# First batch's loads of a rotary attention and feed-forward kernel: 26 transfers where there were 56

## The chip, the cores and the metric

The kernel runs on one core of a Trainium2 chip. The core has a matrix engine (TensorE, PE in the profile), a vector engine (VectorE, DVE), a scalar engine (ScalarE, ACT), GpSimd (POOL) and a queue engine (SyncE, SP) that starts nearly all transfers between the chip's memory and the on-chip memory; 16 DMA engines carry them out. The metric is the device time of one execution in microseconds (us), the median of three runs.

## The reference

Attention with rotated q and k over 4 batches, 8 heads, 576 positions and 64 columns, then a feed-forward layer on the 2304 rows of 512:

```python
def rotate(x):
    x1, x2 = (x[..., :half], x[..., half:])
    return np.concatenate([x1 * cos - x2 * sin, x1 * sin + x2 * cos], axis=-1)
q_rot, k_rot = (rotate(q), rotate(k))
scores = scale * np.matmul(q_rot, k_rot.transpose(0, 1, 3, 2))
scores = scores - np.max(scores, axis=-1, keepdims=True)
attn = np.exp(scores)
attn = attn / (np.sum(attn, axis=-1, keepdims=True) + 1e-09)
attn_out = np.matmul(attn, v)              # then heads side by side: x
h = x @ w_in                               # 512 to 2048
g = h * (1.0 / (1.0 + np.exp(-h)))
out = g @ w_out                            # 2048 to 512
```

All inputs and the output are 32-bit floats. The kernel splits most operands of the matrix engine into a high and a low half-precision part and adds the products.

## The kernel before, in words

The heads of a batch are taken in four pairs, p = 0 to 3. Batches 1 to 3 are split into two half-precision parts and turned by transposing transfers. The first batch goes another way, so that the matrix engine has work early: its q and k are rotated as 32-bit products with the sine and the cosine table (`product`, two instructions for the first 512 positions and one for the last 64 of each table), and the matrix engine turns both products and adds them (`tr`). Its v is needed in two forms: as 32-bit blocks for the first half of the queries (`first_v`, read by `fpv` in `add_pv_first`), and as half-precision parts (`hi`, `lo_first`) for the second half.

The 512 positions are laid out four to a partition, so their transfer is one instruction for two heads; the last 64 positions of each head take transfers of their own. `add_qk_first` issues six transfers for a pair (q, its two last blocks, k, its two last blocks), `add_v` three for v, and `add_v_first` three more for v's second copy: 12 for each of the four pairs. The two rotation tables take four each, the 512 positions twice, so that both heads have a copy. That makes 56.

The weights come in 16 pieces of rows, are rounded by a chain ACT, POOL or ACT, DVE (`fT`, `fC`, `fX`: L811, L813, L819), and their sums of squares give the scales (`trace`, L357 on the matrix engine). The first piece is loaded before anything else, the second behind the tables.

What runs when is written out by hand: `ORDER` is one list of numbered steps, each with the letter of its engine (s for SP's queue). Every engine works through its own steps in that order, and an instruction that waits holds up all behind it on its engine. SP's queue runs eight transfers at a time: each further one waits until the one eight before it has landed. Buffers come from rotating pools (`TAGS`): `rt` and `n` have two each, `io` two, `ob` four, `Tk2` four. Until a weight's place is used for the weight, q, k and v of the first pairs lie in it (`x_place`).

The lines that matter here: L448 and L453 load q and k, L657 to L662 and L628 to L633 load v, L420 and L422 load the tables, L473 and L475 are the rotation's products, L487 to L497 the turning, L813 and L819 the rounding of a weight.

Of the kernel before, what the change touches and what calls it, by code (L numbers as in the profile page):

```python
# [14 lines left out]
ALU = mybir.AluOpType  # L15
# [5 lines left out]
STREAM = (0,)  # L21

# [16 lines left out]
468s 4s 1s 5d 9d 470a 469a 3s 471d 2s 10d 11t 476a 477d 472s 473a 474p 6d 7t 20s 13s 12a 0d 25d 475d 478t 479d 8a 663t  # L39
664d 673t 665a 674d 480t 21p 481d 22p 14t 15d 482d 23t 36s 38d 675a 676t 24d 677d 483p 486p 484a 37d 492s 494a 485d  # L40
45s 46t 47d 26p 493a 678t 495d 679d 666t 667a 27t 680a 52s 39t 40a 28d 61s 488s 42d 62t 29s 63d 681t 496s 41p 487d 57d
43t 54d 490a 683t 53p 682a 35s 30t 31d 489a 58p 684d 73s 19s 497a 498p 668t 685a 669d 75s 68t 69d 70d 670a 686t 671t
687a 499d 71p 502a 16d 491d 503d 55t 44a 18d 500a 501d 504t 672a 32a 48d 50d 505d 64d 514s 506p 507d 688t 510p 56a
689d 508p 74s 690a 693t 694d 1875d 652p 698t 699d 695a 509d 34d 691t 692a 512p 700a 1882d 516a 696t 697a 59t 701t 84d
60d 76a 708t 77a 511p 709d 703t 702a 85d 713t 562s 564a 90p 704d 78t 714d 563a 79d 710a 711t 86p 534s 515a 518s 1876t
513p 91d 1878t 715a 535a 520p 517d 80d 538s 705a 565d 706t 1877d 1879d 712d 536a 92p 537d 716t 723t 724d 707a 718t
1885t 717a 519a 521d 719d 539a 725a 726t 542t 81p 540a 541d 543d 66d 727a 558s 560p 559a 720a 1889d 82d 544a 524t 545d
554s 522t 523d 721t 546t 525d 51s 722a 547d 526t 548p 561d 527d 528d 72d 728t 729d 733t 738t 556a 555a 730a 734d 735a
731t 732a 549p 739d 740a 529p 557d 532p 533d 566a 1890t 530p 736t 1891a 567d 33s 568t 741t 569d 570t 571d 572d 742a
1883t 743t 759t 1880p 1881p 65s 531d 1884a 1886d 573p 1892t 744d 576p 577d 737a 578a 579p 745a 746a 550a 17s 552a 760d  # L50
106s 751t 1896d 1897t 1898a 83d 747d 67s 1899t 1893d 604s 551d 1894d 752d 1895p 653p 748d 93a 1887d 749d 1900d 580s
753a 754d 761a 1888d 605a 94d 762d 755d 763d 1901a 1902p 87a 756a 775t 776d 750s 767t 95s 764a 777a 757d 88p 1987t
778a 768d 769a 783t 121p 553d 1988a 1989d 581a 582a 108a 784d 779d 1994t 765d 89s 770d 785a 584s 799t 780d 766s 1990d
583d 574a 1991d 781d 758s 107a 575d 588a 109t 97s 1995a 1996d 800d 585a 586a 1992t 122p 782s 786a 1997a 587d 115p 801a
2003t 590a 589d 771d 802d 123d 772a 110d 111p 112a 1998d 591d 600s 592t 593d 803d 804a 594p 595a 116d 787d 596a 773d
774s 791t 124p 792d 793a 805d 815t 2004a 597d 1993t 606a 2005d 788a 117d 608s 789d 607d 610p 598a 794a 795d 118a 96s
807t 796p 119d 808d 602a 2010t 1999t 125d 806s 601a 2001t 603d 809a 810a 811d 816d 609a 1903t 2006a 812p 113d 611d
614t 817a 120s 2007d 797d 615d 612a 613d 599d 616t 617d 818d 2002a 98a 831t 618p 2011a 137s 139a 619p 2012d 832d 622a
833a 819d 624a 813p 1904d 1905d 126s 790s 138a 2000a 623d 2013p 823t 820a 824d 825a 798s 630s 814s 2017t 834d 835d
# [131 lines left out]
def rope_attention_silu_ffn(  # L191
# [63 lines left out]
    def buf(tag, *key):  # L255
        if (tag, key) not in live:
            n, shape, dt = TAGS[tag]
            if tag not in pools:
                banks.close()
                for t in ("m1", "m2"):  # L260
                    pools[t] = ctx.enter_context(
                        tc.tile_pool(name="p_" + t, bufs=TAGS[t][0], space=PSUM, reuse_waits="tile")
                    )
            live[tag, key] = pools[tag].tile(shape, dt, tag=tag, name=tag)
        return live[tag, key]

    def bk(tag, *key):
# [1156 lines left out]
```

## Time and profile before

| | |
|---|---|
| median of 3 runs | 623.76 us (622.08 to 627.3) |
| the profiled execution's own time | 620.01 us |
| its span, first to last instruction | 618.2 us |
| TensorE busy | 589.8 us, 95% of the span |
| VectorE, ScalarE, GpSimd busy | 471.3, 403.9, 295.5 us |
| mean granted TensorE clock | 0.989 of full |

The profile gives one execution. Its busy times are sums over the whole span; a stage can have quite another limit than the whole. The slices show the span in 40 equal parts of 15.5 us, a digit for the busy share in tenths. The chain of waits is followed back from the last instruction to what released each step. In a timeline a row is a start, a duration, the engine, the line of the kernel and the operation, and in brackets the idle time ahead of it and what ended it.

### The profile page before, as it was taken

How to read it: one execution, taken by the hardware profiler on the slowest of the kernel's cores; microseconds unless marked ns; L12 is line 12 of the kernel's file. 1: busy time of each engine (PE TensorE's matmuls, PEld its weight loads, DVE VectorE, ACT ScalarE, POOL GpSimd, SP SyncE). 2: the span in 40 equal slices, each digit the busy share in tenths (PEclk: the TensorE clock that was granted, in tenths of full speed). 3: DMA queues.
4: the chain of work that ended last, by engine and by line, in shares of the span. 5: the costliest groups of instructions: out<-in, count | busy, mean ns of one | idle time of the engine just before them, and what ended most of it. 6: DMA issues, size and time to landing. Idle time of an engine off the chain costs nothing.

```text
span 618.2 us, 12511 instructions
## 1 busy us (share of the span) xinstructions
PE 589.8 (95%) x4484; PEld 391.4 (63%) x4484; DVE 471.3 (76%) x1039; ACT 403.9 (65%) x845; POOL 295.5 (48%) x306
## 2 busy tenths in 40 slices
PE   1999898999999999999999999999999999999997
PEld 1776655565566666666676666666666666666663
DVE  3598989999898999999888898897888674322312
ACT  2479889998888877777757786677664653322321
POOL 0549665365744676443755356452556662010131
PEclk9789999989999999999999999999999999999999
DMA  6779449997979899999956899997966655100201
GB/s 194 226 228 375 139 116 212 227 231 157 166 155 204 153 166 168 170 192 175 189 100 151 154 199 166 193 147 130 161 103 113 116 103 95 34 2 2 52 1 34
DMA packets 210671, 91.17 MB, mean 147 GB/s; under 512 B 188465, under 2 KB 194353, under 8 KB 210609
## 3 DMA queue, kind: packets, MB, share of 16 engines
q1 hardware_dynamic: 210448, 90.08, 70.1%
q8 instruction: 35, 0.57, 0.4%
q10 hardware_dynamic: 160, 0.30, 0.3%
q14 instruction: 28, 0.22, 0.1%
HBM read 36.73 MB, written 4.72 MB: 67 GB/s over the span
## 4 chain that ended last, share of the span: by engine, by line
PE 79%; DVE 7%; ACT 5%; DMA 4%; issue 2%; POOL 1%; SPq 1%; POOLq 0%; DVEq 0%; ACTq 0%
PE m L1309 28%; PE m L1252 27%; PE pv L1197 7%; PE s L1095 7%; DMA pt<-pn 2%; PE s L1086 2%; PE s L967 1%; PE s L1101 1%; PE s L980 1%; DMA w_in<-in_q_dram 1%; DMA w_out<-in_moe_w_out_dram 1%; PE mx L1034 1%; ACT e L1129 1%; PE s L487 1%; PE s L357 1%
## 5 line engine op out<-in xcount | busy, mean ns | idle before, releaser
L1252 PEld LDWEIGHTS <-w_in 128*128 128x128 f16 x1728 | 167.3, 98 | 34.0 <-issue 5.1
L1252 PE MATMUL m<-xh,w_in 128*128 128x256 f16 x1024 | 179.7, 274 | 1.8 <-DVE g L1268 1.8
L1309 PE MATMUL m<-w_out,gh 128*128 128x512 f16 x576 | 171.6, 379 | 0.0
L1252 PE MATMUL m<-xl,w_in 128*128 128x256 f16 x512 | 140.2, 274 | 0.0
L1129 ACT ACTIVATE e<-s,small 128x576 f32<-128x576 f32 x128 | 98.5, 770 | 42.0 <-DVE s L1111 19.9
L1309 PE MATMUL m<-w_out,gl 128*128 128x512 f16 x288 | 109.1, 379 | 0.0
L1268 DVE SCALAR_TENSOR_TENSOR g<-g,m 128x512 f32<-128x512 f32 x72 | 49.1, 681 | 60.6 <-ACT g L1264 31.9
L344 DVE SCALAR_TENSOR_TENSOR pn<-e,small,pn 128x576 f16<-128x576 f32 x93 | 82.2, 887 | 6.9 <-ACT pn L338 4.1
L1309 PEld LDWEIGHTS <-gh 128*128 128x128 f16 x576 | 52.0, 99 | 54.5 <-issue 3.9
L1264 ACT ACTIVATE g<-m,small 128x512 f32<-128x512 f32 x64 | 43.7, 682 | 55.6 <-PE m L1252 50.7
L338 ACT ACTIVATE pn<-e,small 128x576 f16<-128x576 f32 x75 | 57.3, 768 | 15.8 <-DVE small L1143 12.4
L1095 PE MATMUL s<-Tk,Tq 128*128 128x512 f16 (+1 forms) x384 | 61.4, 286 | 0.6 <-ACT e L1129 0.5
L1197 PE MATMUL pv<-pt,vh 128*64 128x320 f16 (+1 forms) x504 | 54.1, 290 | 0.0
L332 POOL TENSOR_SCALAR pn<-e,small 128x576 f16<-128x576 f32 x31 | 27.0, 871 | 56.5 <-DVE small L1143 38.1
L1111 DVE TENSOR_SCALAR_CACHE_REDUCE s<-s,small 128x576 f32<-128x576 f32 x59 | 47.9, 817 | 6.2 <-PE s L1095 4.2
L344 DVE SCALAR_TENSOR_TENSOR gl<-g,small,gh 128x512 f16<-128x512 f32 x53 | 43.1, 813 | 11.8 <-ACT gh L338 7.4
L1309 PEld LDWEIGHTS <-gl 128*128 128x128 f16 x288 | 28.2, 98 | 34.0
L347 POOL TENSOR_TENSOR pn<-e,pn 128x576 f16<-128x576 f32 x35 | 45.5, 1300 | 2.9
L1095 PEld LDWEIGHTS <-Tq 128*128 128x128 f16 x384 | 28.9, 99 | 27.0 <-issue 4.2
L1118 DVE TENSOR_REDUCE small<-s 128x1 f32<-128x576 f32 x49 | 36.8, 750 | 9.7 <-PE s L1095 9.5
L332 POOL TENSOR_SCALAR g<-g,small 128x512 f32<-128x512 f32 x19 | 17.0, 894 | 56.4 <-ACT gh L338 37.9
L332 POOL TENSOR_SCALAR e<-e,small 128x576 f32<-128x576 f32 x35 | 28.3, 809 | 30.6 <-ACT pn L338 23.2
(213 smaller groups left out, 1030.1 us busy)
## 6 DMA issues: line engine op xcount, KB each, us to landing
w_in<-in_moe_w_in_dram SPq DMA_DIRECT2D x4, 1024.0 KB, 6.2
w_out<-in_moe_w_out_dram SPq DMA_DIRECT2D x4, 1024.0 KB, 5.6
out_dram<-ob SPq DMA_DIRECT2D x28, 128.0 KB, 2.4
io<-in_q_dram SPq DMA_DIRECT2D x12, 288.0 KB, 3.3
io<-in_k_dram SPq DMA_DIRECT2D x12, 288.0 KB, 3.7
io<-in_v_dram SPq DMA_DIRECT2D x12, 288.0 KB, 4.0
io<-in_v_dram SPq DMA_DIRECT2D x13, 256.0 KB, 4.4
Tk<-Tk SPq DMA_DIRECT2D x22, 144.0 KB, 3.3
```

Of the source, the lines that this page charges most:

```text
L332: e.tensor_scalar(out=out, in0=in0, scalar1=s1, scalar2=s2, op0=ALU.mult, op1=ALU.bypass if s2 is None else ALU.mult)
L338: act.activation(hi, src, AF.Copy, scale=s)
L344: dve.scalar_tensor_tensor(out=lo, in0=src, scalar=s, in1=hi, op0=ALU.mult, op1=ALU.subtract)
L347: e.tensor_tensor(out=lo, in0=src, in1=hi, op=ALU.subtract)
L1095: pe.matmul(o, tq[:, j, 2 * c:2 * c + 2, :], kt[:, r0:r1, js], start=(n == 0), stop=(n == 1))
L1111: dve.tensor_scalar(out=t, in0=t, scalar1=cc[1], scalar2=None, op0=ALU.mult, op1=ALU.min, accum_out=m_of(1, 2),)
L1129: act.activation(buf("e", i), buf("s", i)[:, 0:S], AF.Exp, bias=m_of(1, 2), scale=-1.0 if fused[i] else cc[0], accum_out=m_of(2, 3),)
L1197: pe.matmul(o[64 * j:64 * j + 64, 0:m], vt[part][:, j, s, :], pt[:, a, j, 0:m], start=(z == 0), stop=(z == len(steps) - 1),)
L1252: pe.matmul(t[:, c, 0:n], w[:, wz, kk, fs], xx[:, kk, 0:n], start=(kk == 0 and x == 0), stop=(kk == KD - 1 and x == 2),)
L1264: act.activation(g[:, :, 0:n], t[:, :, 0:n], AF.Tanh, scale=th_v[units[u][0]][:, i:i + 1])
L1268: dve.scalar_tensor_tensor(out=g, in0=g, scalar=1.0, in1=t, op0=ALU.add, op1=ALU.mult)
L1309: pe.matmul(o, gs[gz][:, c, ts], w[:, wz, c], start=(first and c == 0 and x == 0), stop=(last and c == 1 and x == 2),)
```

## The change

All steps keep their engines and their order in the list. These things differ:

- The last 64 positions of q, of k and of v of all eight heads are loaded together into three tiles of the pool `ob` (`x8`, `v5`, `vf5`): two transfers each for q, for k and for v's two forms. Per pair there remain one transfer for q, one for k and one for v.
- v's first 512 positions are loaded once, as 32-bit blocks into `Tk2`; the half-precision parts are now taken from there. `add_v_first` is gone, and v no longer lies in the weights' places or in `io`.
- The tables' 512 positions are loaded once; both heads read the same copy.
- A pair's k is loaded ahead of its q.
- `hi` and `lo_first` become two instructions each, one for the 512 positions and one for the last 64.

New steps `wk` for the matrix engine are defined (`N_KEEP`), and the list gives all 84 the letter z, which issues nothing. The letter A, for ACT's queue, is allowed for some loads and used for none of them.

```diff
-    def load_first(t, src, n):
+    def load_first(e, t, src, n):
         rows = src[0:64].rearrange("p (r d) -> (p r) d", d=n)
         main = rows[0:512].rearrange("(q a) d -> q (a d)", a=4)
+        q_of[e].dma_start(out=t[:, 0:4 * n], in_=main)
         for j in range(2):
-            sp.dma_start(out=t[:, 4 * j * n:4 * (j + 1) * n], in_=main)
-        for j in range(2):
-            sp.dma_start(out=t[64 * j:64 * j + 64, 8 * n:9 * n], in_=rows[512:576])
+            q_of[e].dma_start(out=t[64 * j:64 * j + 64, 8 * n:9 * n], in_=rows[512:576])
...
+    def add_last_blocks():
+        for nm, src in (("q", q), ("k", k)):
+            def ld(e, i="qk".index(nm), src=src):
+                for j in range(2):
+                    q_of[e].dma_start(
+                        out=x8_of()[64 * j:64 * j + 64, i], in_=src[0, j::2, 512:576].rearrange("z p d -> p z d")
+                    )
+            add("x8", (nm,), "sA", ld, [], [bk("ob", "x8")], "x8")
+        def ld5(e):
+            t = v5_of().rearrange("p z j d -> p (z j) d")
+            q_of[e].dma_start(out=t[0:64], in_=v[0, :, 512:576].rearrange("h p d -> p h d"))
+            q_of[e].dma_start(out=t[64:128], in_=v[0, :, 0:256:4].rearrange("h p d -> p h d"))
+        def ldf(e):
+            for h in range(2):
+                q_of[e].dma_start(
+                    out=vf5_of()[64 * h:64 * h + 64], in_=v[0, h::2, 512:576].rearrange("z p d -> p z d")
+                )
...
-        def ld():
-            for i, src in enumerate((q, k)):
-                t = src[0, 2 * p:2 * p + 2]
-                sp.dma_start(
+        for nm in "kq":
+            i = "qk".index(nm)
+            def ld(e, i=i):
+                t = (q, k)[i][0, 2 * p:2 * p + 2]
+                q_of[e].dma_start(
                     out=x()[:, i, 0:8].rearrange("p (j a) d -> p j (a d)", j=2),
                     in_=t[:, 0:512].rearrange("j (r a) d -> r j (a d)", a=4),
                 )
-                for j in range(2):
-                    sp.dma_start(out=x()[64 * j:64 * j + 64, i, 8], in_=t[j, 512:576])
...
-                    eng[e].tensor_tensor(out=dst, in0=x4[:, rs], in1=tab[:, rs], op=ALU.mult)
+                    eng[e].tensor_tensor(out=dst, in0=x4[:, 4 * j:4 * j + 4], in1=tab[:, 0:4], op=ALU.mult)
                 dst = o[:, 512:576].rearrange("p (u d) -> p u d", u=2)
-                eng[e].tensor_tensor(out=dst, in0=x4[:, 8], in1=tab[:, 8], op=ALU.mult)
+                eng[e].tensor_tensor(out=dst, in0=x8, in1=tab[:, 8], op=ALU.mult)
...
         def hi(e):
-            part_hi(eng[e], buf("vh", b, p)[:, :, 0:5] if b == 0 else buf("vh", b, p), f(), st["s"])
+            if b:
+                part_hi(eng[e], buf("vh", b, p), f(), st["s"])
+            else:
+                part_hi(eng[e], buf("vh", b, p)[:, :, 0:4], f(), st["s"])
+                part_hi(eng[e], buf("vh", b, p)[:, :, 4], v5_of()[:, p], st["s"])
...
-            part_lo(dve, vl_t[p], f(), st["s"], buf("vh", b, p)[:, :, 0:5])
+            part_lo(dve, vl_t[p][:, :, 0:4], f(), st["s"], buf("vh", b, p)[:, :, 0:4])
+            part_lo(dve, vl_t[p][:, :, 4], v5_of()[:, p], st["s"], buf("vh", b, p)[:, :, 4])
```

SP's queue from its first transfer to the second piece of the weights, before (x2 is two instructions in a row; `w_in` and `w_out` are the weights' tiles, which hold the first pairs' q and k as well):

```order
L785 DMA w_in<-in_moe_w_in_dram 128x4x512
L448 DMA w_in<-in_q_dram 128x2x256
L453 DMA w_in<-in_q_dram 64x64 x2
L448 DMA w_in<-in_k_dram 128x2x256
L453 DMA w_in<-in_k_dram 64x64 x2
L420 DMA sin_t<-in_sin_dram 128x256 x2
L422 DMA sin_t<-in_sin_dram 64x64 x2
L431 DMA id_t<-in_ident_dram 128x128
L420 DMA cos_t<-in_cos_dram 128x128 x2
L422 DMA cos_t<-in_cos_dram 64x32 x2
L791 DMA w_out<-in_moe_w_out_dram 128x2x1024
```

The same place in the changed kernel:

```order
L818 DMA w_in<-in_moe_w_in_dram 128x4x512
L492 DMA w_in<-in_k_dram 128x2x256
L460 DMA ob<-in_k_dram 64x4x64 x2
L492 DMA w_in<-in_q_dram 128x2x256
L460 DMA ob<-in_q_dram 64x4x64 x2
L429 DMA sin_t<-in_sin_dram 128x256
L431 DMA sin_t<-in_sin_dram 64x64 x2
L440 DMA id_t<-in_ident_dram 128x128
L429 DMA cos_t<-in_cos_dram 128x128
L431 DMA cos_t<-in_cos_dram 64x32 x2
L824 DMA w_out<-in_moe_w_out_dram 128x2x1024
```

Two transfers fewer stand ahead of the second weight piece, one of them ahead of the small sine rows; the four small ones of q and k are four times as wide.

SP's queue just behind that, before (the second pair's q and k, then the first pair's v):

```order
L448 DMA w_out<-in_q_dram 128x2x256
L453 DMA w_out<-in_q_dram 64x64 x2
L448 DMA w_out<-in_k_dram 128x2x256
L453 DMA w_out<-in_k_dram 64x64 x2
L657 DMA w_in<-in_v_dram 128x2x256
```

and in the changed kernel:

```order
L492 DMA w_out<-in_k_dram 128x2x256
L492 DMA w_out<-in_q_dram 128x2x256
L686 DMA Tk<-in_v_dram 128x2x256
L468 DMA ob<-in_v_dram 64x8x64
L469 DMA ob<-in_v_dram 64x8x64
```

The second pair's k is now the first behind the weight and q the second; before, q was the first and k the fourth.

GpSimd's first steps before, with what each waits for (the second pair's k times the sine table; DMAHW names the places in SP's ring of eight):

```order
L813 TENSOR_SCALAR w_out<-w_out 128x1024 [waits DMAHW0_49]
L473 TENSOR_TENSOR rt<-w_out,sin_t 128x4x64 [waits DMAHW4_49,DMAHW7_49,DVE_49,PE_49]
L473 TENSOR_TENSOR rt<-w_out,sin_t 128x4x64
L475 TENSOR_TENSOR rt<-w_out,sin_t 128x64 [waits DMAHW5_49,DMAHW6_49,DMAHW2_49,DMAHW1_49]
L473 TENSOR_TENSOR n<-w_out,cos_t 128x4x64 [waits DVE_49]
```

and in the changed kernel:

```order
L846 TENSOR_SCALAR w_out<-w_out 128x1024 [waits DMAHW6_49]
L515 TENSOR_TENSOR rt<-w_out,sin_t 128x4x64 [waits DMAHW7_49,DVE_49,PE_49]
L515 TENSOR_TENSOR rt<-w_out,sin_t 128x4x64
L517 TENSOR_TENSOR rt<-ob,sin_t 128x64 [waits DMAHW2_49,DMAHW3_49,DMAHW1_49,DMAHW0_49]
L515 TENSOR_TENSOR n<-w_out,cos_t 128x4x64 [waits DMAHW3_49,DVE_49]
```

The steps are the same. The first of the products now waits for the place of k's single transfer right behind the weight.

## Rows read from the trace of the kernel before

**Rows 1.** The page: busy time by engine (share of span, instructions); the 40 slices.

```profile
PE 589.8 (95%) x4484; PEld 391.4 (63%) x4484; DVE 471.3 (76%) x1039; ACT 403.9 (65%) x845; POOL 295.5 (48%) x306
...
PE   1999898999999999999999999999999999999997
```

**Rows 2.** Chain of waits, first 21 us: start, duration, what ran.

```profile
11.37 5.18 DMA w_out<-in_moe_w_out_dram
...
18.48 1.15 DVE w_out L819
...
19.68 1.11 PE mx L357 x8
```

**Rows 3.** SP's timeline: start us, us, engine, line, operation, out and in, count.

```profile
5.03 2.04 SPq L420 DMA_DIRECT2D sin_t<-in_sin_dram  x2
7.48 1.11 SPq L422 DMA_DIRECT2D sin_t<-in_sin_dram  x2
...
11.37 0.58 SPq L791 DMA_DIRECT2D w_out<-in_moe_w_out_dram  x1
12.00 0.47 SPq L448 DMA_DIRECT2D w_out<-in_q_dram  x1
...
13.68 0.59 SPq L448 DMA_DIRECT2D w_out<-in_k_dram  x1
```

**Rows 4.** Transfers issued up to 5.1 us: count, KB, us from issue to landing.

```profile
w_in<-in_q_dram SPq DMA_DIRECT2D x1, 256.0 KB, 6.2
...
sin_t<-in_sin_dram SPq DMA_DIRECT2D x1, 128.0 KB, 3.7
```

**Rows 5.** Transfers issued from 11.3 to 16 us.

```profile
w_out<-in_moe_w_out_dram SPq DMA_DIRECT2D x1, 1024.0 KB, 5.2
w_out<-in_q_dram SPq DMA_DIRECT2D x1, 256.0 KB, 5.4
w_out<-in_k_dram SPq DMA_DIRECT2D x1, 256.0 KB, 4.6
```

**Rows 6.** Packets from 8 to 8.45 us, and their share of 16 engines.

```profile
DMA packets 133, 0.12 MB, mean 266 GB/s; under 512 B 16, under 2 KB 133, under 8 KB 133
...
q1 hardware_dynamic: 133, 0.12, 77.0%
```

**Rows 7.** Packets from 8.7 to 9.4 us.

```profile
DMA packets 85, 0.02 MB, mean 25 GB/s; under 512 B 85, under 2 KB 85, under 8 KB 85
...
q1 hardware_dynamic: 85, 0.02, 11.8%
```

**Rows 8.** VectorE timeline; in brackets idle time before and its releaser.

```profile
8.84 0.76 DVE L473 TENSOR_TENSOR rt<-w_in,sin_t 128x256 f32<-128x256 f32 x2 [8.84 <-DMA sin_t<-in_sin_dram]
10.17 0.22 DVE L475 TENSOR_TENSOR rt<-w_in,sin_t 128x64 f32<-128x64 f32 x1 [0.57 <-issue]
...
17.47 0.88 DVE L473 TENSOR_TENSOR rt<-w_out,sin_t 128x256 f32<-128x256 f32 x2 [3.39 <-DMA w_out<-in_q_dram]
...
36.38 0.75 DVE L475 TENSOR_TENSOR rt<-io,sin_t 128x64 f32<-128x64 f32 x1
37.05 1.43 DVE L473 TENSOR_TENSOR n<-io,cos_t 128x256 f32<-128x256 f32 x2
38.41 0.75 DVE L475 TENSOR_TENSOR n<-io,cos_t 128x64 f32<-128x64 f32 x1
...
47.82 1.42 DVE L972 TENSOR_REDUCE small<-s 128x1 f32<-128x576 f32 x2 [0.43 <-PE s L967]
```

**Rows 9.** GpSimd's timeline.

```profile
16.63 1.11 POOL L813 TENSOR_SCALAR w_out<-w_out 128x1024 int32<-128x1024 uint16 x1 [16.21 <-DMA w_out<-in_moe_w_out_dram]
18.50 2.41 POOL L473 TENSOR_TENSOR rt<-w_out,sin_t 128x256 f32<-128x256 f32 x2 [0.75 <-DVE rt L475]
...
36.19 1.54 POOL L473 TENSOR_TENSOR rt<-io,sin_t 128x256 f32<-128x256 f32 x2 [2.23 <-issue]
```

**Rows 10.** Busy us by stretch and engine, granted TensorE clock, DMA share, GB/s.

```profile
20.00:30.00 10.00, 10.00 (x54) 7.78 (x53) 5.30 (x17) 3.90 (x7) 6.12 (x11) 0.66 0.77 216
```

More of the change, by code (lines that the diff above doesn't have):

```diff
@@ L21 @@
 STREAM = (0,)
+N_KEEP = 84
 RAW_PLACE = [
@@ L44 @@
[L44 to L53, printed above, removed]
@@ L434, in rope_attention_silu_ffn, with load_ident, x8_of, v5_of @@
+    def load_ident(e):
+        q_of[e].dma_start(out=id_t, in_=ident)
     qk = {}
     turn = {"q": "s3", "k": "s"}
+    def x8_of():
+        return buf("ob", "x8").rearrange("p (i z d) -> p i z d", i=2, z=NP)
+    def v5_of():
+        return buf("ob", "v5").rearrange("p (z j d) -> p z j d", z=NP, j=2)
+    def vf5_of():
+        return buf("ob", "vf5")[:, 0:64 * NP].rearrange("p (z d) -> p z d", z=NP)
+    def add_last_blocks():
[15 more added lines that the diff above has]
+                )
+        add("v5", (), "sA", ld5, [], [bk("ob", "v5")], "v5")
+        add("vf5", (), "sA", ldf, [], [bk("ob", "vf5")], "vf5")
@@ L466, in turned, with x8, product @@
                 return buf("n", 0, p, nm).rearrange("p r d -> p (r d)").bitcast(F32)
-            def product(e, which, x4, tab, turned):
+            def x8(i=i):
+                return x8_of()[:, i, p].rearrange("p (u d) -> p u d", u=2)
+            def product(e, which, x4, x8, tab, turned):
                 o = turned(which)
@@ L1355, in add_step, with add_keep, f @@
                     add("st", (u, tt), "s", fst, [o_], [obb], it)
-    pl.add(("ones",), "d", lambda: dve.memset(ones, 1.0))
-    pl.add(("sin0",), "s", load_sin_first)
-    pl.add(("cos0",), "s", load_cos_first)
-    pl.add(("ident",), "s", load_ident)
+    pl.add(("ones",), "dp", lambda e: eng[e].memset(ones, 1.0))
+    ones_b = ones.bitcast(BF16)[:, 0:128]
+    def add_keep(z):
+        def f(e):
+            if e == "t":
+                if "wk" not in live:
+                    buf("s3", "wk")
+                o = live["wk"][:, 640:1024].rearrange("p (a n) -> p a n", a=3)
+                for _ in range(2):
+                    pe.matmul(o, ones_b, ones_b[:, None, :].to_broadcast([128, 3, 128]), start=True, stop=True)
+        return add("wk", (z,), "zt", f, [("ones",)])
+    keep = [add_keep(z) for z in range(N_KEEP)]
+    pl.add(("sin0",), "sA", load_sin_first)
+    pl.add(("cos0",), "sA", load_cos_first)
+    pl.add(("ident",), "sA", load_ident)
+    add_last_blocks()
     for b in range(B):
```

318 lines of the change are left out of this document (159 added, 159 removed).

## The prediction

> **What bounds the kernel now.** I read the page first: TensorE is busy for 589.8 of 618.2 us, and of the 40 slices only the first, a few behind it and the last are below full [rows 1]. So 28.4 us of the span are TensorE's idle time, and most of that stands at the start, where the change is. A microsecond won or lost there goes through to the end, because TensorE, once it has work, is the engine that is waited for.
>
> The chain of waits says what the start waits for [rows 2]: SP's issues until the second weight piece is issued at 11.37 us, that transfer, its rounding on ACT, VectorE's last rounding step (the chain is on it from 18.48 us, for 1.15 us, to 19.63), and at 19.68 us TensorE's sums of squares. In VectorE's timeline [rows 8] three waits stand ahead of that: 8.84 us until the sine table is there, 0.57 us until its last rows are there, and 3.39 us until 17.47 us, for the second pair's q. The last is the one to watch, since the rounding step is queued behind it: the products of that q take 0.88 us for the two large ones and about 0.2 for the small one.
>
> **The parts of the change.** *Ahead of the first products.* The profile gives a price for a packet. From 8.0 to 8.45 us nearly all packets were of 1 KB: 133 of them for 77.0% of 16 engines, so 0.77 x 0.45 x 16 / 133 = 41.7 ns each [rows 6]. From 8.7 to 9.4 us all were small: 85 for 11.8%, 15.5 ns each [rows 7]. The first of the 256 KB transfers took 6.2 us to land [rows 4], and the small sine rows were issued at 7.48 us [rows 3], when its place in the ring came free; the first sine transfer, issued at 5.03 us, took 3.7 us and landed at 8.73. Between the two landings lay 384 packets of 1 KB and 256 small ones, by the two prices 1.25 us, which is what the trace has (8.73 - 7.48). In the changed kernel the four small transfers carry all heads: 1024 small packets instead of 256. That makes 1.99 us, and the sine table lands at 9.47 us: 0.74 us later. The second copy of the table and one issue fall away, so its last rows are issued no later than now and are there when VectorE has done the two large products. VectorE begins at 9.58 and is at the small product at 9.58 + 0.76 - 0.08 (rows overlap by that much) = 10.26 us, where it is now at 10.17 [rows 8]. The idle 0.57 us is gone and the start is 0.74 later: **+0.1 us**. If the wide transfers start no slower than the narrow ones and the sine lands as now, it is -0.6; if a small packet costs as much as a large one, the landing moves by 768 x 41.7 / 16 = 2.0 us and the term is +1.4.
>
> *The second weight piece.* From 7.48 to 11.37 us SP issued 7 transfers, 0.556 us each [rows 3]. Now 5 lie between: the issue comes at 7.48 + 5 x 0.556 = 10.26 us, 1.1 us earlier, and lands after the same 5.2 us [rows 5] at 15.46 instead of 16.57. By itself **-1.1 us**, if that landing were what ends last.
>
> *The order behind it.* It isn't. The second pair's q landed at 12.00 + 5.4 = 17.40 us and its k at 13.68 + 4.6 = 18.28 [rows 3, 5]: steps of 0.83 and 0.88 us behind the weight. Now k comes first, at 16.29, and q second, at 17.1: VectorE's wait ends at about 17.17 instead of 17.47, a gain of 0.3. But GpSimd, which multiplies k, began that at 18.50 us, just when VectorE had finished q [rows 9]. With the weight's landing its own rounding, 1.11 us, ends at 16.6, k is there by then, and it begins its six products at 16.6. The four large ones of these take two by two at least 1.54 us [rows 9], so it is at them until past 19.7: across all of VectorE's products of q.
>
> What that costs shows where both engines multiply at once. From 36.38 to 39.16 us, with GpSimd's products running from 36.19, VectorE needs 0.75 us for a small product that takes 0.22 alone, 1.43 for two large ones that take 0.76, and 0.75 for another small one [rows 8, 9]: 0.70 us per instruction. Three such make 2.1 us: q's products end at 19.27 and not at about 18.48, and the rounding step behind them, some 1.2 us, ends at 20.5; with half of a large GpSimd product to wait for, at 20.85. Now it ends at 19.63. I take the middle, **+1.1 us**, and this contains the gain of 0.3, the start's +0.1 and the unused 1.1 us. Ends: -0.4 (no collision, the landing of q decides), +2.8 (each engine waits out the other, below).
>
> The Trainium skill, "SBUF — State Buffer", section "Who interferes with whom", says that a VectorE instruction with two inputs in the on-chip memory contends with a GpSimd instruction that reads there, and that whoever comes first holds the pair of ports for the whole instruction. The stretch at 36 us agrees that they slow each other, but not fully: four VectorE and most of six GpSimd instructions fit into 2.78 us, fewer than their times alone add up to. By the rule in full the term would be +2.8, by the row +1.1.
>
> *Splits.* `hi` and `lo_first` add seven instructions on VectorE and one on ACT. A large product takes 0.38 us, a small one 0.22 [rows 8]: 0.00083 us per element, so 0.17 us for an instruction as such, 1.2 us for seven. Five of them lie ahead of 47.82 us, where VectorE still idles 0.43 us for TensorE [rows 8], and the later two lie between waits of the same kind. I take 0; without that cover +0.8.
>
> *Fewer issues, v once, weights no longer behind v.* 30 issues of 0.556 us leave SP's queue and four waits of weight loads on v's last readers go. The loads land some microseconds earlier, but the waits by engine show VectorE and TensorE waiting for no load of this batch past 20 us but a fraction for one block of v: 0; at best -0.5, at worst nothing lost, since the table's second load, which stays behind the rotations, holds the queue as now.
>
> *Sum.* 620.0 us (the profiled execution's own time) + 1.1 = 621.1. That execution was 3.7 us below the median of the runs shown, so against the median **624.9 us**. One per cent, 6.2 us, is about what a measurement here can tell from no change; this forecast is no change.
>
> **Rivals.**
> - *No collision (0.30).* For it: GpSimd's first product needs a free buffer as well as k, and may come second again. Then q's landing decides, -0.4: 623.4; if q lands with the weight's whole advance, -1.1: 622.7.
> - *A faster clock (0.12).* From 20 to 30 us TensorE had 0.66 of its clock on the mean and was busy for all 10 us [rows 10]: 6.8 us of it at 1.2 GHz, the rest at 2.4. This followed an idle piece ahead of 19.68. If TensorE's first work, shifted, leaves it at 2.4 GHz, half of 6.8 us comes back: +1.1 - 3.4 = -2.3, 621.5; without the collision 620.0. Against it: the idle time ahead of the sums of squares grows in the forecast.
> - *A slower clock (0.10).* The other side: with the idle time longer by the collision, 2.4 us and more, TensorE stays at 1.2 GHz for as long again as now: +3.4, with the collision and uncovered splits +5.3: 629.1. It decides if the granted clock from 30 to 40 us falls clearly below 1.
> - *The engines wait each other out (0.08).* Each of the three products waits for a whole large GpSimd one (1.54 / 2 = 0.77 us) and then takes its own time, 0.98 us for all three [rows 8, 9]: 3 x 0.77 + 0.98 = 3.3 us, the rounding waits 0.77 more and ends at 22.4: +2.8, 626.6. Against it: the stretch at 36 us is shorter than that.
> - That the change doesn't do what it says is no case: SP's list holds the 26 transfers, and the new TensorE steps issue nothing.
>
> **Numbers.** The forecast has the remaining 0.40. Each case scatters by some 1.5 us, as the runs shown do. From 620.0 to 628.5 lie the forecast, no collision, the waiting out, most of the faster clock and half of the slower one. Faster by over 1% (below 617.5) needs the faster clock and more: 0.05. Slower by over 1% (above 630.0) needs the slower clock with a late sine table: 0.07. The rest, 0.88, is within 1%.
>
> **What would show it.** VectorE's first product at 9.6 us and its small one at 10.2 to 10.3 without idle time between; the second weight piece issued at 10.3 and landed at 15.5; GpSimd's first product of k at 16.6; VectorE's products of q from 17.2 and its three instructions 2 us long, not 1.1; the sums of squares at 20.8. I am wrong if GpSimd begins behind VectorE there, if the granted clock of the stretches from 20 to 50 us is another, or if time moves behind 130 us, where I expect the old picture, shifted.

## The result, and the profile after

The changed kernel takes 619.48 us (median of 15 runs, 617.61 to 628.02), the kernel before 624.41 (15 runs, 622.08 to 630.19) on the same chip. The ratio is 0.9905, 95% interval 0.9877 to 0.9934: 0.7 to 1.2% faster. The forecast was 624.9 us and no change. Run again beside `e6` to `e8` it gave 0.9954 (0.9923 to 0.9984). Over both sets its executions have a median span of 617.8 us and a mean granted clock of 0.989 (25 executions); 160 timed executions of the kernel before have 622.0 us and 0.985. Two executions of each kernel that ran over 1.5% longer than its fastest are left out of these figures. None of the 160 is below 618.5 us, and 17 of the 25 are.

The two profiles hardly differ in length: 618.2 us before, 618.0 after. The profiled execution of the kernel before was quicker than any of its 160 timed ones, so what it does is not what the kernel usually does. That was the trap in this case.

The page (as [rows 1]):

```profile
PE 589.6 (95%) x4484; PEld 391.1 (63%) x4484; DVE 473.0 (77%) x1046; ACT 404.7 (65%) x846; POOL 293.7 (48%) x306
...
PE   1999998999999999999999999999999999999997
```

SP's timeline of the changed kernel (as [rows 3]):

```profile
6.27 1.55 SPq L431 DMA_DIRECT2D sin_t<-in_sin_dram  x2
...
10.12 0.59 SPq L824 DMA_DIRECT2D w_out<-in_moe_w_out_dram  x1
10.75 0.47 SPq L492 DMA_DIRECT2D w_out<-in_k_dram  x1
11.26 0.47 SPq L492 DMA_DIRECT2D w_out<-in_q_dram  x1
...
19.40 0.37 SPq L818 DMA_DIRECT2D ring<-in_moe_w_in_dram  x1
19.86 0.45 SPq L686 DMA_DIRECT2D Tk<-in_v_dram  x1
```

The second weight piece goes out at 10.12 us (before 11.37), and the last two rows, which weren't in the forecast's argument, are the next 1 MB of input weights (the expectations call them those of the second piece) and v of heads 2 and 3. In the kernel before those weights were issued here:

```profile
29.59 0.59 SPq L785 DMA_DIRECT2D ring<-in_moe_w_in_dram  x1
```

From issue to landing (as [rows 5]):

```profile
w_out<-in_moe_w_out_dram SPq DMA_DIRECT2D x1, 1024.0 KB, 5.2
w_out<-in_k_dram SPq DMA_DIRECT2D x1, 256.0 KB, 5.4
w_out<-in_q_dram SPq DMA_DIRECT2D x1, 256.0 KB, 5.6
```

VectorE, GpSimd and TensorE of the changed kernel (as [rows 8], [rows 9], and the sums of squares in [rows 2]); in brackets idle time ahead and what ended it:

```profile
9.74 0.76 DVE L515 TENSOR_TENSOR rt<-w_in,sin_t 128x256 f32<-128x256 f32 x2 [9.74 <-DMA sin_t<-in_sin_dram]
10.42 0.22 DVE L517 TENSOR_TENSOR rt<-ob,sin_t 128x64 f32<-128x64 f32 x1
...
16.98 0.76 DVE L515 TENSOR_TENSOR rt<-w_out,sin_t 128x256 f32<-128x256 f32 x2 [2.65 <-DMA w_out<-in_q_dram]
17.66 0.22 DVE L517 TENSOR_TENSOR rt<-ob,sin_t 128x64 f32<-128x64 f32 x1
17.80 1.22 DVE L852 SCALAR_TENSOR_TENSOR w_out<-w_out 128x1024 int32<-128x1024 int32 x1
...
15.43 1.12 POOL L846 TENSOR_SCALAR w_out<-w_out 128x1024 int32<-128x1024 uint16 x1 [15.01 <-DMA w_out<-in_moe_w_out_dram]
19.01 1.43 POOL L515 TENSOR_TENSOR rt<-w_out,sin_t 128x256 f32<-128x256 f32 x2 [2.45 <-DVE w_out L852]
...
18.50 0.42 PE L539 MATMUL s<-id_t,rt 128*64 128x128 f32 x1
19.07 1.11 PE L365 MATMUL mx<-w_out 128*128 128x128 bf16 x8 [0.15 <-DVE w_out L852]
20.11 1.57 PE L1000 MATMUL s<-Tk,Tq 64*128 64x64 f32 x10
```

GpSimd, ready at 16.55 us, begins its products of k only at 19.01: right behind TensorE's second turning, which ends at 18.92 and leaves it the buffer that it writes. VectorE's rounding ends at 19.02, too, and the row names that as the releaser. A second profile of the changed kernel, `e5_changed_again`, tells the two apart: there the turning ends at 18.35, and GpSimd begins 0.09 us behind it, in the middle of the rounding.

```profile
18.02 1.22 DVE L852 SCALAR_TENSOR_TENSOR w_out<-w_out 128x1024 int32<-128x1024 int32 x1
...
18.44 2.09 POOL L515 TENSOR_TENSOR rt<-w_out,sin_t 128x256 f32<-128x256 f32 x2 [1.79 <-PE s L539]
...
18.08 0.27 PE L539 MATMUL s<-id_t,rt 128*64 128x128 f32 x1
19.30 1.10 PE L365 MATMUL mx<-w_out 128*128 128x128 bf16 x8 [0.95 <-DVE w_out L852]
```

(In the kernel before the turning's last row ends at 18.35, and GpSimd begins at 18.50.) So it meets none of VectorE's products of q, and the sums of squares begin at 19.07 instead of 19.68, with 0.15 us idle ahead of them instead of 1.32. Only half of these 1.17 us come from the rounding, which ends 0.6 us sooner. The other half is the turning, which ends 0.57 us later than in the kernel before: its last row takes 0.42 us in this execution, and 0.27 in that of the kernel before and in `e5_changed_again`, where TensorE stands idle for 0.95 us. The first scores behind the sums take 1.57 us; in the kernel before, in its profile, 2.53.

Stretches (as [rows 10]), the changed kernel and then one of the kernel before:

```profile
20.00:30.00 10.00, 10.00 (x80) 7.80 (x79) 8.66 (x21) 4.50 (x8) 7.42 (x12) 1.00 0.82 291
...
40.00:50.00 10.00, 9.94 (x36) 7.02 (x36) 6.64 (x17) 6.71 (x16) 4.51 (x11) 0.50 1.01 385
```

```profile
40.00:50.00 10.00, 9.11 (x54) 7.16 (x53) 8.48 (x18) 8.48 (x19) 4.22 (x9) 0.83 0.75 250
```

From 20 to 30 us TensorE has 2.4 GHz throughout (0.66 of it before). VectorE's pair of reductions at 36.90 us stands at 39.29 in the kernel before: 2.4 us of lead. Then, in this execution, the clock is at 1.2 GHz from 40 us on (0.50; before 0.83), and at 59.68 us VectorE is level again (59.56 before). Behind 130 us both run the same steps in the same time: VectorE's steps of 133.30 and 133.97 us stand there in both.

### The profile page after: what moved, and what is told of

It is laid out like the page before. It is cut to its first block, busy times and chain, and to the rows that moved or that the text cites. A ratio compares the mean times of both kernels' runs of the same rounds, so it can differ in the third digit from the quotient of the medians.

```text
span 618.0 us, 12474 instructions
## 1 busy us (share of the span) xinstructions
PE 589.6 (95%) x4484; PEld 391.1 (63%) x4484; DVE 473.0 (77%) x1046; ACT 404.7 (65%) x846; POOL 293.7 (48%) x306
## 4 chain that ended last, share of the span: by engine, by line
PE 74%; DVE 8%; ACT 7%; DMA 5%; issue 3%; SPq 1%; POOL 1%; ACTq 0%; POOLq 0%; DVEq 0%
PE m L1342 27%; PE m L1285 26%; PE s L1128 7%; PE pv L1230 7%; DMA pt<-pn 2%; PE s L1000 2%; ACT e L1162 1%; PE s L1134 1%; DMA w_in<-in_k_dram 1%; DMA vh<-vh 1%; DMA w_out<-in_q_dram 1%; ACT pn L346 1%; DVE small L1149 1%; DVE pn L352 1%; PE s L1013 1%
## 5 line engine op out<-in xcount | busy, mean ns | idle before, releaser
L340 POOL TENSOR_SCALAR g<-g,small 128x512 f32<-128x512 f32 x19 | 16.4, 863 | 56.1 <-ACT gh L346 37.6
```

Of the source, the lines that this page charges most:

```text
L340: e.tensor_scalar(out=out, in0=in0, scalar1=s1, scalar2=s2, op0=ALU.mult, op1=ALU.bypass if s2 is None else ALU.mult)
```

## The experiments

Path theory: the second weight piece comes sooner, and that is the gain. Clock theory: TensorE spends less time at 1.2 GHz. Gap theory: it does so because its idle time ahead of the first sums of squares is shorter. Late-load theory: the long queue of the kernel before made somebody wait at 30 to 40 us. Ratios are to the kernel before on the same chip, with 95% intervals.

### Is the clock in it? Both kernels again, and all parts undone

`e1_before_again` and `e5_changed_again` are the two kernels unedited.

> The kernel before, unchanged, run for its clock and span in every execution (so far only its times are known, 622 to 630 us, and one profile of 620.0 us). Clock theory: most of the 5 us that the changed kernel gained is time that TensorE no longer spends at its low clock; then the mean granted clock of this kernel's executions is about 0.980 (some 10 us more at half clock than the 0.988 of the changed kernel, each us of it worth half a us), and longer spans go with lower clocks. Path theory: a step of the chain is shorter in every execution; then the mean clock is the same 0.988 and the spans are still 621 to 624 us.

> The changed kernel, unchanged, on the same chip as the three that follow. If its gain is a property of the kernel: ratio 0.9905 again (0.988 to 0.993), mean clock about 0.9885 against 0.985 of the kernel before, and spans of 616 to 618 us in the executions with a clock of 0.988 or more, where the kernel before has 620.3. If it was a matter of the chip or the hour: a ratio nearer 1.000, as the two parts undone singly gave.

Measured: 1.0012 (0.998 to 1.0043) and 0.9954 (0.9923 to 0.9984). The clock theory is right about the kernel before: mean clock 0.985, and its span falls with the clock, by 2.5 us per 0.010 (a line through 47 executions). But its executions with a clock of 0.988 or more still take 620.7 us on the mean, those of the changed kernel 617.2. So the clock is part of it, and probably not all. The mean clock is a rough measure, though: `e16` below reads 1.00 from 20 to 30 us, and its first scores take 2.88 us all the same, as in `e17`, which reads 0.50 there. A slow start can be missing from the mean.

```profile
20.00:30.00 10.00, 10.00 (x52) 7.84 (x51) 5.50 (x17) 3.90 (x7) 5.65 (x10) 1.00 0.72 207
...
20.27 2.88 PE L1008 MATMUL s<-Tk,Tq 64*128 64x64 f32 x10
```

The profile of `e5_changed_again` is the fairest comparison of the two starts, since the clock did in it what it did in [rows 10]:

```profile
20.00:30.00 10.00, 10.00 (x55) 7.84 (x53) 5.71 (x17) 3.91 (x7) 5.73 (x10) 0.66 0.78 280
40.00:50.00 10.00, 8.87 (x51) 6.71 (x50) 8.75 (x23) 8.55 (x20) 4.04 (x9) 0.83 0.97 347
```

Its span is 617.7 us: 0.5 us below 618.2. In this pair of executions that is what the change is worth with the clock alike, near the rival "no collision" (-0.4).

`e2_all_undone`:

```diff
-        q_of[e].dma_start(out=t[:, 0:4 * n], in_=main)
+        for j in range(2):
+            q_of[e].dma_start(out=t[:, 4 * j * n:4 * (j + 1) * n], in_=main)
...
+            g, fb = x_place(b, p, "v")
...
+                out=first_v(p)[:, 0:512].rearrange("p (j d) -> p j d", j=2),
...
+                if p:
+                    rows8(e, i, p)
...
-556s 92s 89s 97s 88s 85s
+556s 97s 88s 92s 89s 85s
```

(The tables twice; v into the weights' buffers, with a second load for the products; the last rows in each pair's own step; and q ahead of k, here the first pair's entries of the order.)

> The changed kernel with all four parts of its loads undone at once: tables twice, q ahead of k, v loaded twice, the last rows of q, k and v pair by pair. What stays of the change is the tile for the last rows and the operations split because of it. All theories that put the gain down to the loads expect the time of the kernel before (ratio 1.000, 0.997 to 1.003). If the split operations or the tile bring or cost something, it shows here: a ratio of 0.991 would say that the loads had no part in it, one of 1.003 or more that the splits cost 2 us or more.

Measured 1.0005 (0.9978 to 1.0031). The splits and the extra tile cost and bring nothing that can be seen, so the gain is in the loads.

### One part undone at a time

Each is one of the four edits above.

> The changed kernel with v loaded twice again: the first copy into the places in the weights' buffers where the steps on v read it, the second copy later for the products with v. Theory that the freed places matter (the weights' loads of pieces 2 to 4 no longer wait for the steps on v, and went out at 37 to 41 us where they went at 44 to 53): the gain is gone, ratio 0.997 to 1.003. Path theory (only the second piece of weights and its place in the queue matter, which this leaves alone): ratio 0.991 as for the changed kernel. Clock theory: in between, by what TensorE's clock then does.

> The changed kernel with the second copies of the sine and cosine tables loaded again: two more transfers of 128 KB and 64 KB ahead of the second piece of weights on the queue. Path theory: that piece is issued some 1.0 us later (10.1 to 11.1 us) and lands at about 16.3, VectorE's rounding of it and the first sums of squares move from 17.8 to about 18.4 us, and the 0.6 us are lost: the time is 0.6 us up, ratio 0.992 if that is all, up to 0.997 if the whole gain hangs on the early start. Clock theory: what the clock does between 15 and 60 us decides; a shift of 0.6 us alone is not enough, the mean clock tells. Theory of the freed places: no difference from the changed kernel, 0.991.

> The changed kernel with q loaded ahead of k again in the four pairs; nothing else differs, in number or in bytes. Theory that the place of k matters (VectorE's first product is of k, and GpSimd's first products are of k): the first product begins when both are there either way, since the sine rows come behind both, so no difference there; of the second pair k lands some 0.5 us later, but GpSimd begins its products on it only at 19.0 us. So 0.9905 as the changed kernel (0.988 to 0.994). Clock theory: the same unless TensorE's start moves; if the ratio comes out near 1.000, the gain is so sensitive that any shift of the first 20 us loses it.

> The changed kernel with the last rows of q, k and the first place of v loaded pair by pair again (12 small transfers more of 16 KB, 6 more of v; each holds the queue for about 0.6 us). Theory of the late v: the queue gets to v of heads 2 and 3 some 8 us later (28 instead of 20 us), it lands at 33 to 35 us, and most of the gain is lost: ratio 0.997 to 1.000. Path theory (only the second weights' piece counts; one fewer row transfer lies ahead of it or the same): 0.991 to 0.995.

Measured: v twice 0.9986 (0.9954 to 1.0019), tables twice 1.0014 (0.9988 to 1.004), q first 0.9969 (0.9939 to 0.9999), last rows apart 1.0009 (0.9974 to 1.0044). Nothing adds up: with two transfers of tables put back nothing is left of the gain, with eighteen small ones neither, and with v twice little. Several of the expectations missed. Two limits: the changed kernel itself was run again beside `e6` to `e8` alone, so what it would have given beside the others isn't known; and beside it (0.9954) q first can't be told from it. A gain that each of several parts takes away is not a sum of parts; it looks like one that needs conditions that hold together. In the profile of the tables twice the first is seen:

```profile
20.25 1.11 PE L365 MATMUL mx<-w_out 128*128 128x128 bf16 x8 [1.27 <-DVE w_out L853]
```

The second weight piece is late again, the gap is 1.27 us, and from 20 to 30 us the clock is 0.66, although no engine waits for a load from 22 to 42 us.

### Holding the clock up

A step that the changed kernel lists but never issues was made to issue pairs of 128x384 bf16 products that nobody reads (for the kernel before it was copied in):

```diff
+        for _ in range(2):
+            pe.matmul(o, ones_b, ones_b[:, None, :].to_broadcast([128, 3, 128]), start=True, stop=True)
```

> The kernel before, with 27 pairs of 128x384 bf16 products that nobody reads added to TensorE, and the ones they read written first: 18 pairs ahead of its first turning (from about 1 to 12 us, when TensorE has nothing to do), 4 ahead of the first sums of squares (its gap at 18 to 19.7 us), 3, 1 and 1 in its later gaps up to 55 us. Clock theory (the whole gain is low-clock time saved): with the clock up the kernel before is as quick as the changed one or quicker, span about 616 or less, ratio 0.990 or below, mean clock 0.992 or more. Theory of a second bound (the executions of the kernel before with the best clock, 0.993 and 0.994, lie at 620.3 us, no less than some with 0.989): the clock goes up and the time stays at about 620, ratio 0.995 to 0.998. Path theory: the same, since the path does not go through TensorE's turnings.

> The changed kernel with the same 27 pairs of products in the same places. Clock theory: the same time as the kernel before with them, within 0.3%. Theory of a second bound that the change lifts: 3 to 4 us less than that, span 615 to 616 us, ratio about 0.988, which is what its own executions with a clock of 0.994 have (615.8 to 616.3). If the products delay work that waits for TensorE, both are slower by the same amount.

> The kernel before with 44 such pairs, placed so that no gap opens: 31 ahead of the first turning (up to 13 us; the 18 of the earlier run ended at 8.9 us, and the clock fell at 11 us), 7 ahead of the first sums of squares, 2, 1, 2 and 1 in the later gaps up to 50 us. Clock theory: no low clock from 5 to 55 us, span about 615, ratio 0.988, and the same as the changed kernel with them but for 0.6 to 1 us. Second-bound theory: 619 to 620, ratio 0.995 to 0.997, with the clock up.

> The changed kernel with the same 44 pairs in the same places. Clock theory: span 613 to 615, ratio 0.985 to 0.988, 0.6 to 1 us below the kernel before with them, since only its own start is left as a difference. Second-bound theory: 3 to 4 us below it. If the pairs overrun the gaps and delay the work behind them, both are no quicker than without them.

Measured: 1.0036 (1.0009 to 1.0064) and 1.0016 (0.999 to 1.0042) with 27 pairs, where the clock fell at 11 us behind the last early pair; 1.0007 (0.998 to 1.0034) and 0.9998 (0.997 to 1.0025) with 44, with a mean clock of 0.989 and 0.990. The clock is as high as in the changed kernel, and nothing is gained. That speaks against the clock theory alone, but doesn't settle it, because the pairs also delay work: the sums of squares begin at 20.56 and 21.32 us with 27 pairs and at 22.30 and 20.90 with 44, where they begin at 19.68 and 19.07 without. What else the pairs cost is seen in `e12_changed_warm_2`, VectorE and GpSimd:

```profile
17.40 1.50 DVE L494 TENSOR_TENSOR rt<-w_out,sin_t 128x256 f32<-128x256 f32 x2 [3.29 <-DMA w_out<-in_q_dram]
18.81 0.34 DVE L496 TENSOR_TENSOR rt<-ob,sin_t 128x64 f32<-128x64 f32 x1
19.07 1.77 DVE L831 SCALAR_TENSOR_TENSOR w_out<-w_out 128x1024 int32<-128x1024 int32 x1
...
17.02 1.59 POOL L494 TENSOR_TENSOR rt<-w_out,sin_t 128x256 f32<-128x256 f32 x2
...
19.04 2.40 POOL L494 TENSOR_TENSOR n<-w_out,cos_t 128x256 f32<-128x256 f32 x2
```

TensorE turns the first pair at 2.4 GHz and is done at 16.4 us, GpSimd has its buffer and begins at 17.02, and this is the forecast's collision: VectorE's three products and the rounding take 3.44 us instead of 2.04, and the rounding ends at 20.84 us, where the forecast had 20.5 to 20.85. In the two profiles of the changed kernel the turning ends too late for it, at 18.92 and 18.35 us.

### The gap alone, and the tables alone, in the kernel before

`e9_before_gap` puts 3 such pairs ahead of the first sums of squares (478); `e10_before_tables_once` loads the tables once:

```diff
-478t
+2531t 2532t 2533t 478t
...
-        for j in range(2):
-            sp.dma_start(out=t[:, 4 * j * n:4 * (j + 1) * n], in_=main)
+        sp.dma_start(out=t[:, 0:4 * n], in_=main)
```

> The kernel before with 3 pairs of 128x384 bf16 products that nobody reads in TensorE's gap ahead of the first sums of squares (1.32 us idle at 18.4 to 19.7 us in its profile); nothing else. Gap theory: what the change gained is that this gap is shorter (0.15 us idle in its profile), so that the clock seldom falls at 20.6 to 22.2 us (it fell there in the profiles of the kernel before, of all parts undone and of the tables twice; it did not in that of the changed kernel, of v twice and of q first). Then the filled gap gives most of the gain to the kernel before: span mean about 619.5, ratio 0.996, mean clock 0.988. Path theory (the transfers as such, sooner on the path): no gain, ratio 1.000 to 1.001, where the pairs overrun the gap.

> The kernel before with the sine and cosine tables loaded once, all other loads as before: two transfers fewer ahead of the second piece of weights. Gap theory: that piece comes about 1 us sooner, the gap on TensorE is 0.3 to 0.6 us instead of 1.3, and part of the gain comes with this edit alone: ratio 0.996 to 0.998. If the freed places of v, the merged rows or k ahead of q are needed: 1.000.

Measured 1.0004 (0.9978 to 1.003) and 1.0014 (0.9989 to 1.004). Both did to the clock what they should: in both profiles it is 1.00 from 20 to 30 us and the first scores take 1.57 us. `e10_before_tables_once`, TensorE and then ScalarE:

```profile
18.59 1.10 PE L357 MATMUL mx<-w_out 128*128 128x128 bf16 x8 [0.48 <-DVE w_out L818]
19.62 1.57 PE L966 MATMUL s<-Tk,Tq 64*128 64x64 f32 x10
...
36.87 0.29 PE L357 MATMUL pv<-w_out 128*128 128x128 bf16 x2 [1.70 <-DMA w_out<-in_v_dram]
...
35.99 1.13 ACT L810 ACTIVATE ring<-ring 128x1024 int32<-128x1024 uint16 x1 [4.36 <-DMA ring<-in_moe_w_in_dram]
```

It is 1.1 us ahead of the kernel before at the sums, and then ScalarE stands 4.36 us for the next input weights and TensorE 1.70 us for v of heads 2 and 3. In `e9_before_gap` the same two waits are 3.89 and 1.16 us. This is the late-load theory: the kernel before can't use an early TensorE. Its own profile has that wait, too, which I had overlooked:

```profile
35.79 1.16 ACT L811 ACTIVATE ring<-ring 128x1024 int32<-128x1024 uint16 x1 [1.62 <-DMA ring<-in_moe_w_in_dram]
```

### Single transfers moved

In the kernel before, v of heads 2 and 3 ahead of the weights (alone in e13, with the tables once in e14); in the changed kernel, that v late (e15), or the weights late (e17):

```diff
-61s 488s
-29s
+61s 29s 488s
...
-118s
+118s 119t
...
-576s
+576s 578a
```

(29 and 118 load v of heads 2 and 3, 488 and 576 the weights; the first edit is of the kernel before, the others of the changed one. e15 also gets one more transfer of 256 KB ahead of that v, which isn't in the lines shown; so it changes two things.)

> The kernel before with the load of v of heads 2 and 3 (three transfers) put ahead of the 1 MB of weights that it follows; nothing else. Theory of the late v: it lands some 3 to 4 us sooner (about 33 us), TensorE no longer waits for it where it is early, and executions of 617 to 618 us appear; those in which the clock fell at 21 us are late anyway and gain nothing. Span mean about 621, ratio 0.997 to 0.999. Clock or gap theory: 1.000.

> The kernel before with both: the tables once (alone: 1.0014) and v of heads 2 and 3 ahead of the weights. Theory of the late v: the tables once bring TensorE forward (2.2 us ahead at 26 us in its profile, lost again at 37 us in the wait for v), and now it keeps it: ratio 0.993 to 0.996, most of the gain of the change with two small edits. If the theory is wrong: 1.000 as with each alone.

> The changed kernel with the load of v of heads 2 and 3 put at the end of the first loads, behind the last rows of v (issued at about 30.5 us), with one more transfer of the same 256 KB ahead of it to a place that nobody reads, so that it lands at about 36 to 37 us as in the kernel before. Nothing else is undone. Theory of the late v: the gain is gone, ratio 0.998 to 1.000, no execution below 618.5 us. If the gain comes from the start (second weights' piece, gap at 18 us): 0.991 to 0.995 as before.

> The changed kernel with the 1 MB of input weights of the second piece (issued at 19.4 us in its profile, in the kernel before at about 29.5) put behind the half MB that follows it, so that it is issued at about 29 us and lands at about 35.5. The start is not touched. If both locks are needed: ScalarE waits 2 to 4 us for it (its conversion begins at 35.5 to 36.5 us), the lead at 37 us is lost, ratio 0.998 to 1.001, although the first scores take 1.57 us in most executions. If the start alone matters: 0.991 to 0.995.

Measured: 1.0056 (1.0022 to 1.0091), 1.0026 (0.9996 to 1.0057), 1.0015 (0.9986 to 1.0045), 1.0000 (0.9965 to 1.0035). The first two missed: putting v ahead put the weights back, and ScalarE's wait for them became 4.27 us in the profile of the first. With the queue of the kernel before, the weights came 2.56 to 4.36 us late in the four profiles in which TensorE was early or v was put ahead (e9, e10, e13, e14). The other two came out as expected in time: with either transfer late in the changed kernel, no gain is seen. For e17 there is a near control: e18 below, run beside it, has 0.9919. In the profile of the last one ScalarE waits again, but the gap and the low clock (0.50 from 20 to 30 us) are there too, so this profile doesn't keep the two apart:

```profile
38.04 1.16 ACT L823 ACTIVATE ring<-ring 128x1024 int32<-128x1024 uint16 x1 [1.28 <-DMA ring<-in_moe_w_in_dram]
...
19.22 1.11 PE L344 MATMUL mx<-w_out 128*128 128x128 bf16 x8 [1.21 <-DVE w_out L831]
```

### The gap closed in the changed kernel

```diff
-114d 563d 566t
+563d 114d 566t
```

VectorE rounds the second weight piece (563) ahead of its product of q (114).

> The changed kernel with VectorE's rounding of the second piece of weights (1.22 us) ahead of its two products on q of the second pair and their small one (0.76 and 0.22 us), for which it now waits 2.65 us. ScalarE and GpSimd have done their part on the weights at 16.5 us, so the rounding runs at 16.6 to 17.8 instead of 17.8 to 19.0, and the first sums of squares begin as soon as TensorE has turned the first pair (about 18.5): no gap ahead of them in any execution. Theory of the two locks: the clock falls less often at 21 us; ratio 0.988 to 0.992, span mean 617 to 618. If the gap doesn't matter: 0.992 to 0.994 as the changed kernel. If q of the second pair, then 1.2 us later, is what TensorE waits for at 27 us: slower than the changed kernel.

Measured 0.9919 (0.9884 to 0.9954), median 618.39 us, the lowest of all; mean clock 0.991, and 9 of 11 executions at 0.990 or more. It was not run beside the changed kernel, and the intervals overlap: that it is quicker than that one is likely, not shown. VectorE, TensorE, and a stretch:

```profile
16.71 1.23 DVE L831 SCALAR_TENSOR_TENSOR w_out<-w_out 128x1024 int32<-128x1024 int32 x1 [2.47 <-POOL w_out L825]
...
18.11 1.10 PE L344 MATMUL mx<-w_out 128*128 128x128 bf16 x8
19.14 1.57 PE L979 MATMUL s<-Tk,Tq 64*128 64x64 f32 x10
```

```profile
40.00:50.00 10.00, 9.10 (x58) 6.58 (x57) 8.96 (x22) 8.80 (x19) 6.41 (x10) 0.94 1.03 399
```

### All profiles side by side

The sixteen profiles without pairs ahead of the turning: TensorE's idle time ahead of the first sums of squares, what the first scores took, and the longest wait of an engine for a load between 22 and 42 us.

| profile | idle, us | first scores, us | wait for a load, us | span, us |
|---|---|---|---|---|
| before | 1.32 | 2.53 | 1.62 | 618.2 |
| e1 before again | 2.35 | 2.73 | 1.37 | 625.1 |
| e2 all undone | 2.21 | 2.88 | none | 625.9 |
| e13 | 1.22 | 2.88 | 4.27 | 624.7 |
| e14 | 2.48 | 2.88 | 2.56 | 626.6 |
| e16 last rows apart | 1.28 | 2.88 | 1.15 | 623.4 |
| e17 weights late | 1.21 | 2.88 | 1.28 | 623.4 |
| e4 tables twice | 1.27 | 2.06 | none | 619.0 |
| e5 changed again | 0.95 | 2.68 | none | 617.7 |
| e10 tables once | 0.48 | 1.57 | 4.36 | 623.4 |
| e9 gap filled | 0.79 | 1.57 | 3.89 | 622.6 |
| e15 v late | 0.38 | 1.57 | 0.26 | 622.0 |
| changed | 0.15 | 1.57 | none | 618.0 |
| e8 q first | none | 1.57 | none | 619.4 |
| e3 v twice | 0.17 | 1.57 | none | 615.8 |
| e18 round first | none | 1.57 | none | 615.0 |

In each of the nine with the longer idle time the first scores ran, in part or whole, at 1.2 GHz; in the seven others at 2.4. Where only one of the two columns is good, the kernel is no quicker than before (e9, e10; e4, over 12 executions). Both are good in the first profile of the changed kernel (in e5 one is), and the lowest spans, 615.0 and 615.8 us, are two of the four with both good to the full.

The table leaves out what the clock does later, and that differs as much. From 40 to 50 us it is 0.50 in the changed kernel and 0.84, 0.85 and 0.94 in e3, e8 and e18. From 60 to 130 us it is 1.00 in the changed kernel, 0.93 in e8 and e16, 0.96 in e15, and 0.98 before. In e8 a reduction of VectorE is 2.1 us ahead of the kernel before at 54.23 us and 1.3 us behind it at 136.10; in e16 it is level at 56.23 us and 3.2 us behind at 137.98. e15 keeps pace with the changed kernel's own profile up to 57.43 us (57.56 there), whatever its late v does, and is 3.0 us behind it at 77.44, with a clock of 0.83 from 60 to 70 us. So these three profiles lose their time while the clock is low, where no engine waits for a load that the kernel before doesn't wait for as well; that the edits bring the low clock about isn't shown.

## Why the prediction was wrong

Point by point:

- **Start, +0.1.** The first product is at 9.74 us (forecast 9.58 in the sum), the small one at 10.42 without idle time: +0.25. Right in kind.
- **Second weight piece, -1.1.** Issued at 10.12 us (10.26), landed by 15.4 (15.46). Right in the sum, by two errors that cancel: the small sine rows went out at 6.27 us, over a microsecond sooner than before, and from there six issues took 0.64 us each, not 0.556.
- **The collision, +1.1: the step that failed first.** That "it begins its six products at 16.6" took GpSimd to wait for k and its own rounding alone. It also waits for the buffer that TensorE's second turning reads, as the rival "no collision" had it at 0.30. [rows 9] could not decide it: GpSimd was idle until 18.50, the turning ended at 18.35, and VectorE's last product, which the row names as releaser, at 18.48; I read it as VectorE's. Without the collision the chain moved by -0.6 (19.07 against 19.68). Where the collision does come, in `e12_changed_warm_2`, it ends the rounding at 20.84 us; the total was right, but its parts were not (three products 1.75 us instead of 2.1, the rounding 1.77 instead of 1.2 to 1.6).
- **Fewer issues, 0: as far as the runs show, the step that cost most.** "VectorE and TensorE waiting for no load" left ScalarE out, which waited 1.62 us for weights in the same trace, and costed the queue by what was covered in that execution. The cover was TensorE's low clock from 20 to 30 us. Take it away and the wait is 3.9 to 4.4 us (e9, e10). The shorter queue gains nothing by itself (e4 has no such wait and 1.0014); in the changed kernel the weights are issued at 19.40 us instead of 29.59, and no engine waits for a load from 22 to 42 us, so that TensorE can stay early. That both conditions are needed together is argued from these runs, not shown: e17's time speaks for it (1.0000), but its profile has the gap and the low clock as well.
- **The clock.** The rival had the right mechanism at 0.12, and its "against" (the idle time grows) rested on the collision. The idle time shrank from 1.32 to 0.15 us, and in the second profile of the changed kernel to 0.95. The part of it that the clock's own rise during the turning decides was in neither the forecast nor the rival. Closing the gap by order (e18) gave 0.9919.
- **The +3.7 to the median.** Adding a fixed distance supposed that an execution of 620.0 us and one of 624 differ by nothing that the change touches. They differ by the clock in the first 75 us or so, which it touches: the two profiles of the kernel before, 618.2 and 625.1 us long, are 6.3 us apart by then (reductions at 73.95 and 80.26 us).
- **Splits, 0.** Right, as far as can be seen (e2, 1.0005).

What stays open: how much of the gain each of the two conditions holds, the short gap and the early loads (e17's profile doesn't keep them apart); why v late (e15) gains nothing, when its profile shows 0.26 us of waiting for it and its lead goes while the clock is low; and why v twice, with both columns good in its profile, has executions from 615.8 to 624.7 us.

## What to carry to other kernels

Before a stall or a queue is costed at nothing, name what covers it and whether the same change, or another execution, can take that cover away; list the waits of every engine, ScalarE's too. Where executions of one kernel differ by 1% through the clock, a single profile is one draw: compare profiles whose clocks did the same, and time many executions. A gain that any one of several undone parts takes away may hang on conditions that hold together, so test them as pairs, each time with the unedited changed kernel beside them.

## What the runs showed of the hardware

- The granted clock in the first 60 us differs from one execution of the same kernel to the next: from 20 to 30 us it was 1.00 in one profile of the changed kernel and 0.66 in another. The Trainium skill, "TensorE: Matmul & The Clock Gate", section "Part 1: The HAM clock gate", says that the moment at which the clock changes varies from run to run for the same kernel. The two profiles agree in that, though the idle time ahead differed as well (0.15 and 0.95 us).
- More TensorE work is not more clock: with 27 added pairs the mean was 0.983 and 0.982 (without them, beside these runs, 0.987 and 0.989), and the clock fell in the gap behind the early ones; with 44 it was 0.989 and 0.990.
- VectorE and GpSimd slow each other where both multiply, and the one that begins second is slowed. In the kernel before, the rounding begins at 18.41 us and takes 1.21 us; GpSimd's two products of 18.50 us take 2.41 us instead of 1.43. In `e12_changed_warm_2` GpSimd's products begin at 19.04 us, and the rounding of 19.07 takes 1.77 us instead of 1.22. The Trainium skill, "SBUF — State Buffer", section "Who interferes with whom", says that whoever comes first holds the pair of ports for the whole instruction; these two cases agree to 0.15 us (by it GpSimd's products would take 1.12 us of waiting and 1.43 of their own, the rounding 0.69 and 1.22). The forecast's +2.8 by that rule was too much because it let each of VectorE's three products wait for a whole product of GpSimd.

```profile
18.41 1.21 DVE L819 SCALAR_TENSOR_TENSOR w_out<-w_out 128x1024 int32<-128x1024 int32 x1
```
